# A gated dynamic convolution in fp32: output matmuls split around the value matmuls, softmax loads cut by lane, equal short end groups

## The chip, the cores and the metric

One core of a Trainium2 chip runs the program. Its time is the device time of one execution in microseconds (us), lower is better. Five engines run side by side, each in its own program order: PE (TensorE, matmuls; PEld is its weight load), DVE (VectorE), ACT (ScalarE), POOL (GpSimd) and SP (SyncE, which here only issues DMAs). Sixteen DMA engines carry all transfers.

## The reference

`x` is (8, 4224, 192) fp32, `weight_gen` is (8, 4224, 8 heads, 7 taps). The seven taps of each position and head go through a softmax and weight the last seven positions of that head's 24 channels. The result `a` then goes through a gate and two matrix products:

```python
w = softmax(weight_gen, axis=-1)                       # 7 taps
a[b, s, h, :] = sum_k w[b, s, h, k] * x[b, s - 6 + k, h, :]
gate_pre[s]   = sum_j conv_w[j] * a[s - 4 + j]          # 5 taps, per channel
out = (sigmoid(gate_pre) * (a @ w_val)) @ w_out         # 192 x 192 each
```

## The kernel before

The sequence is cut into 36 **groups** of positions, all eight batches ("lanes") of a group together. Before, group 0 has 24 positions and the other 35 have 120 (`N0`, `starts`, L52).

*Softmax.* `weight_gen` is loaded in seven **parts** of 16 x R positions (`Softmax`, L183; R is 10, 14, 30, 30, 60, 60, 60). A part lies on 128 partitions with R + 6 positions of each. `load` (L198) issues it as one DMA per 16 or 8 chunks, the lanes as the outermost dimension: on SP for the first three parts, on POOL for the last four (two DMAs each for the 60s). DVE does max, subtract, sum, reciprocal and normalise in cuts of about 22 positions (`jobs`), ACT the exponential. `spread` (ACT, L254) writes the weights with zeros between them into `zt`, and `store` (L271) writes `zt` to a DRAM block. A block written for the first time gets whole rows of 736 B, zeros and all; one written again gets only the 288 B of data in each row. Of the 60-position parts, part 4 writes fresh blocks and parts 5 and 6 write used ones.

*A group's front.* `load_x` brings positions of `x`, `load_t` the skewed rows of a block into `tb` as eight DMAs onto 16 partitions each; both are issued by SP. `tb` is then a banded matrix. `bank` (PE, L331) multiplies it with `x`, 128 short matmul records for the four banks; `evac` (ACT) takes a bank to the rings `ringA` (128 channels) and `ringB` (64), and `move` (POOL, 12 DMAs) brings the strips of heads 6 and 7 to their places.

*A group's back, one group later.* `tap0` (ACT) and four `tap`s (DVE) for each of the channel groups A and B make `gate_pre`; `sigm` (ACT) the gate; `val` (PE, L403) the product with `w_val`; `gv` (DVE) the product of the two. Then, another group later, `omm(0)` and `omm(1)` (PE, L429), the two **output parts**, four lanes each, multiply with `w_out` into `po`, of which there is one buffer; `oev` (ACT, L458) copies `po` to `ot`, and `store` (SP, L463) writes it out. So `omm(1)` can start only when `oev(0)` has emptied `po`.

*Order.* The program is written with an explicit plan: `at(t, f)` and `stage(m, offset, f)` give each call a time, and the calls are made in the order of those times. Only the order on each engine survives; an engine takes its next instruction when that one's inputs are there. Before, PE's order in a group is bank, val, omm(0), omm(1) (`stage` offsets 0 to 2.8, 3.7, 8.3, 10.7 in L622 to L642). SP's order at a stage is `load_x`, eight `load_t`, then the output stores, with the z stores between. SP issues a DMA only when an earlier one of the same semaphore has landed; eight semaphores go round.

*Weights.* `w_val`, `w_out` and `conv_w` come as 64-bit words and are converted in 8 steps each on DVE and POOL (`convert_weights`, L125).

Of the kernel before, what the change touches and what calls it, by code (L numbers as in the profile page):

```python
# [7 lines left out]
FP32 = mybir.dt.float32  # L8
# [9 lines left out]
def tile_dynconv_gated_moe(  # L18
# [21 lines left out]
    P = 128  # L40
# [11 lines left out]
    N0 = S % NB  # L52
    starts = [0] + [N0 + NB * i for i in range(S // NB)]
# [11 lines left out]
    ZR = 14  # L65
# [113 lines left out]
    blocks = [Block(16 * 10, "za"), Block(16 * 14, "zb")] + [Block(480, f"z{i}") for i in range(4)]  # L179
# [3 lines left out]
    class Softmax:  # L183
# [3 lines left out]
        def __init__(self, r0, R, into, step):  # L187
            self.r0, self.R, self.n = r0, R, R + PAD
            self.into = into
            h = -(-self.n // 22)  # L190
            self.cut = [(self.n * k // h, self.n * (k + 1) // h) for k in range(h)]
            self.zc = [(c, min(c + step, R)) for c in range(0, R, step)]
            self.q = 16 // len(into)
            for i, b in enumerate(into):
                assert b.n == self.q * R
                where.append((r0 + i * self.q * R, b))

        def load(self):  # L198
            R, n, q = self.R, self.n, self.q
            self.wt = wpool.tile([P, self.ROWS, H, K], FP32, name="wt")[:, 0:n]  # L200
            self.mx = wpool.tile([P, self.ROWS, H], FP32, name="mx")[:, 0:n]
            flat = self.wt.rearrange("p r h k -> p (r h k)")
            eng = nc.sync if self.r0 < 864 else nc.gpsimd
            ends = self.r0 + 16 * R == S
            for i in range(len(self.into)):
                off = wg.offset + (self.r0 + i * q * R) * ROW
                p0 = i * L * q

                def part(l0, dims, np, c0, c1):
                    src = bass.AP(tensor=wg.tensor, offset=off + l0 * S * ROW + c0 * ROW,  # L210
                                  ap=[*dims, [1, (c1 - c0) * ROW]])
                    p = p0 + l0 * q
                    eng.dma_start(out=flat[p:p + np, c0 * ROW:c1 * ROW], in_=src)

                every = [[S * ROW, L], [R * ROW, q]]
                if ends and i == len(self.into) - 1:
                    nc.vector.memset(self.wt[P - Q:P, R:], 0.0)
                    part(0, every, L * q, 0, R)
                    part(0, [[S * ROW, L - 1], [R * ROW, q]], (L - 1) * q, R, n)
                    part(L - 1, [[R * ROW, q - 1]], q - 1, R, n)  # L220
                else:
                    part(0, every, L * q, 0, n)
# [48 lines left out]
        def store(self, c):  # L271


            a, b = self.zc[c]
            for i, blk in enumerate(self.into):
                d0 = blk.t[0, a, :]
                p = slice(i * L * self.q, (i + 1) * L * self.q)
                np = L * self.q
                if self.old[i]:
                    dst = bass.AP(tensor=d0.tensor, offset=d0.offset, ap=[[self.R * PITCH, np], [PITCH, b - a], [1, DATA]])  # L280
                    nc.sync.dma_start(out=dst, in_=self.z[p, 0:b - a, 0:DATA])
                else:
                    dst = bass.AP(tensor=d0.tensor, offset=d0.offset, ap=[[self.R * PITCH, np], [1, (b - a) * PITCH]])
                    nc.sync.dma_start(out=dst, in_=self.z[p, 0:b - a].rearrange("p r c -> p (r c)"))

        def begin(self):
            self.old = [b.used for b in self.into]
            for b in self.into:
                b.used = True


    class Group:

        def __init__(self, m):
# [5 lines left out]
            self.p0 = HALO + NB * (m % 3) + NB - self.n  # L300
# [373 lines left out]
```

## Time and profile before

| what | before |
|---|---|
| time, median of 3 runs | 636.42 us (636.29 to 644.36) |
| profiled execution, time | 636.85 us |
| its span, first to last instruction | 634.9 us |
| PE busy | 507.0 us, 80% |
| DVE / ACT / POOL busy | 420.8 / 323.8 / 263.8 us |
| DMA bytes moved | 112.02 MB, 176 GB/s mean |

The span leaves out 1.95 us of the execution's time. A busy share is an average over a start-up, some thirty like groups and an end, so what sets the time has to be read stage by stage. "DMA share" is the mean busy share of the 16 DMA engines by the packets' own durations; packets overlap a little, so it can pass 1. "PEclk" is the granted TensorE clock as a share of full speed.

### The profile page before, as it was taken

What the parts mean: (1) busy time and instruction counts of PE and PEld (TensorE: products, weight loads), DVE (VectorE), ACT (ScalarE), POOL (GpSimd) and SP (SyncE); (2) the same over time, 40 slices, a digit from 0 to 9 for tenths busy, and PEclk for the clock granted to TensorE, in tenths of its full rate; (3) what the DMA queues carried; (4) which work ended last, traced back from release to release, by engine and by line L of the source; (5) the groups of instructions that cost most, each with busy time, mean ns of one, the idle gap of its engine ahead of it and who ended that gap; (6) DMA issues with size and microseconds to landing.
All of it is one profiled execution on the core that took longest, in us unless ns stands there. A gap on an engine that the chain in (4) does not pass through costs nothing. (4 is left out here: it accounts for less than half of the span.)

```text
span 634.9 us, 15917 instructions
## 1 busy us (share of the span) xinstructions
PE 507.0 (80%) x6324; PEld 334.1 (53%) x6324; DVE 420.8 (66%) x470; ACT 323.8 (51%) x521; POOL 263.8 (42%) x474
## 2 busy tenths in 40 slices
PE   7022799598986873999998569999998899999985
PEld 4022545465553553665565445655655566665553
DVE  7263386578886852788888375788885565566661
ACT  7031366455693632469566433694655444554431
POOL 7544244244444421445544252455444444445510
PEclk9556789899999876999999798999999999999998
DMA  6838479989869998687889894778897777777413
GB/s 161 184 113 181 89 250 179 203 219 246 188 127 202 256 242 242 139 178 162 192 196 214 182 229 112 165 166 192 194 207 179 165 166 165 182 167 164 111 53 93
DMA packets 128829, 112.02 MB, mean 176 GB/s; under 512 B 38742, under 2 KB 125922, under 8 KB 127604
## 3 DMA queue, kind: packets, MB, share of 16 engines
q1 hardware_dynamic: 112964, 96.33, 64.2%
q0 software_dynamic: 15792, 14.68, 11.4%
q8 instruction: 50, 0.82, 0.6%
q14 instruction: 23, 0.19, 0.1%
HBM read 60.46 MB, written 44.54 MB: 165 GB/s over the span
## 5 line engine op out<-in xcount | busy, mean ns | idle before, releaser
L369 POOL DMA_DIRECT2D ringA<-S x288 | 155.8, 548 | 265.5 <-ACT ringA L361 205.8
L396 DVE SCALAR_TENSOR_TENSOR aA<-ringA,wf,aA 128x960 f32<-128x960 f32 (+1 forms) x144 | 170.7, 1185 | 137.8 <-ACT aA L389 128.4
L342 PE MATMUL pa<-tb,xt 126*32 126x120 f32 (+1 forms) x4608 | 145.1, 286 | 71.6 <-DMA out_dram<-ot 34.4
L342 PEld LDWEIGHTS pa<-tb,xt 126*32 126x32 f32 (+1 forms) x4608 | 134.7, 118 | 81.2 <-issue 47.1
L461 ACT COPY ot<-po 120x768 f32<-120x768 f32 (+1 forms) x72 | 57.8, 802 | 186.0 <-PE po L440 141.2
L440 PE MATMUL po<-wf,aA 128*120 128x192 f32 (+1 forms) x576 | 114.0, 342 | 32.3 <-ACT ot L461 32.3
L440 PEld LDWEIGHTS po<-wf,aA 128*120 128x120 f32 (+1 forms) x576 | 91.6, 188 | 52.4 <-ACT ot L461 43.2
L371 POOL DMA_DIRECT2D ringB<-S x144 | 78.1, 547 | 61.6 <-DMA ringA<-S 34.5
L396 DVE SCALAR_TENSOR_TENSOR aB<-ringB,wf,aB 128x480 f32<-128x480 f32 (+1 forms) x144 | 101.3, 704 | 2.8 <-ACT aB L389 1.7
L411 PE MATMUL v<-ringA,wva 128*128 128x480 f32 (+1 forms) x144 | 68.9, 600 | 9.1 <-DMA ringA<-S 9.1
L447 PE MATMUL po<-wf,aB 64*120 64x192 f32 (+1 forms) x576 | 66.6, 349 | 2.1 <-DVE aB L427 2.1
L425 DVE TENSOR_TENSOR aA<-v,aA 128x960 f32<-128x960 f32 (+1 forms) x36 | 40.8, 1134 | 36.9 <-ACT aA L401 36.7
L447 PEld LDWEIGHTS po<-wf,aB 64*120 64x120 f32 (+1 forms) x576 | 44.6, 183 | 36.2 <-issue 33.6
L269 ACT COPY zt<-wt 128x192 f32<-128x192 f32 (+2 forms) x92 | 37.5, 487 | 35.0 <-DVE wt L252 35.0
L414 PE MATMUL v<-ringB,wvb 64*128 64x480 f32 (+1 forms) x144 | 43.2, 622 | 6.2 <-DMA ringB<-S 6.2
L389 ACT ACTIVATE aA<-ringA,wf 128x960 f32<-128x960 f32 (+1 forms) x36 | 39.2, 1089 | 17.0 <-DMA ringB<-S 16.6
L361 ACT COPY S<-pa 128x480 f32<-128x480 f32 (+1 forms) x36 | 19.9, 553 | 47.4 <-PE pa L342 47.4
L411 PEld LDWEIGHTS v<-ringA,wva 128*128 128x128 f32 x144 | 25.1, 196 | 32.5 <-issue 30.3
L419 PE MATMUL v<-ringB,wvd 128*128 128x480 f32 (+1 forms) x72 | 39.1, 626 | 0.0
L417 PE MATMUL v<-ringA,wvm 128*64 128x480 f32 (+1 forms) x144 | 37.3, 598 | 0.9 <-DVE aB L427 0.9
L361 ACT COPY ringA<-pa 128x480 f32<-128x480 f32 (+1 forms) x72 | 35.9, 546 | 1.2 <-PE pa L342 1.2
L401 ACT ACTIVATE aA<-aA 128x960 f32<-128x960 f32 (+1 forms) x36 | 35.6, 990 | 1.1 <-DVE aA L396 1.0
(60 smaller groups left out, 337.8 us busy)
## 6 DMA issues: line engine op xcount, KB each, us to landing
xt<-in_x_dram SPq DMA_DIRECT2D x35, 756.0 KB
out_dram<-ot SPq DMA_DIRECT2D x140, 180.0 KB
tb<-z SPq DMA_DIRECT2D x192, 88.0 KB
z<-zt SPq DMA_DIRECT2D x6, 920.0 KB
z<-zt SPq DMA_DIRECT2D x10, 552.0 KB
wt<-in_weight_gen_dram POOLq DMA_DIRECT2D x5, 924.0 KB, 15.3
ringA<-S POOLq DMA_DIRECT2D x280, 15.0 KB, 4.7
z<-zt SPq DMA_DIRECT2D x20, 216.0 KB
```

The lines of the kernel that those rows point to most:

```text
L342: nc.tensor.matmul(out=pa[Q * c:Q * c + Q, n * l:n * l + n], lhsT=self.xb[0:k, LH * u + l, C * h:C * h + Q], rhs=self.t[0:k, LH * u + l, P ...
L361: nc.scalar.copy(out=dst, in_=pa)
L369: nc.gpsimd.dma_start(out=ringA[q:q + h, LH * u:LH * u + LH, p0:p0 + n], in_=self.S[p:p + h])
L371: nc.gpsimd.dma_start(out=ringB[HD * u + q:HD * u + q + h, :, p0:p0 + n], in_=self.S[p:p + h])
L389: nc.scalar.activation(out=self.lanes(self.acc(g)), in_=self.src(g, 0), func=AF.Copy, scale=cw[:, g, 0:1])
L396: nc.vector.scalar_tensor_tensor(out=a, in0=self.src(g, j), scalar=cw[:, g, j:j + 1], in1=a, op0=ALU.mult, op1=ALU.add)
L411: nc.tensor.matmul(out=v01[:, u, 0:w], lhsT=wva, rhs=A[u], start=True, stop=False)
L414: nc.tensor.matmul(out=v01[:, u, 0:w], lhsT=wvb[hs], rhs=Bt[hs], start=False, stop=True, tile_position=(HD * u, 0))
L425: nc.vector.tensor_tensor(out=a, in0=self.v01[:, :, 0:w], in1=a, op=ALU.mult)
L440: nc.tensor.matmul(out=po[0:n, u, D * t:D * t + D], lhsT=gA[:, u, k, t], rhs=woa, start=first and t == 0, stop=not first, skip_group_check ...
L447: nc.tensor.matmul(out=po[0:n, u, D * t:D * t + D], lhsT=gB[hs, k, t], rhs=wob[hs], start=first and t == 0, stop=not first, skip_group_che ...
L461: nc.scalar.copy(out=self.ot[0:n], in_=self.po[0:n, :, 0:2 * D])
```

## The change

The short end groups become equal: `N0` is 72, so the groups have 72, 34 times 120, and 72 positions; there are still 36. The parts become R = 12, 16, 28, 28, 60, 60, 60, each with one block of its own, except that part 6 reuses part 4's block. So part 5 now writes whole rows. A fresh store is cut into runs of four rows (2,944 B) where it was one run of 10 or 12 rows (7,360 or 8,832 B).

A part is loaded lane by lane: eight DMAs of 16 partitions instead of one or two, all on SP (part 0 on SP and ACT in turn). The last three parts are also cut into three by position, so 24 DMAs, in three successive stages.

PE's order in a group becomes bank, omm(0), val, omm(1). `tap`s of B and A alternate; both `sigm` and both `gv` now fall into the group's own back stage, where B's came one later. Bank order is 3, 2, 0, 1 for 3, 0, 1, 2. The softmax jobs and the z stores get new places (three places for a store in a stage instead of two), and the start-up is written out by hand.

```diff
-    N0 = S % NB
+    N0 = (S % NB + NB) // 2
...
+    ZR = 12
+    ZQ = 4
...
+    blocks = [Block(16 * R, f"z{i}") for i, R in enumerate((12, 16, 28, 28, 60, 60))]
...
+        def load(self, l, c0, c1, eng):
...
+            src = wg.offset + (l * S + self.r0) * ROW
...
+                    s = bass.AP(tensor=wg.tensor, offset=src + c0 * ROW, ap=[[R * ROW, q], [1, (c1 - c0) * ROW]])
+                    eng.dma_start(out=flat[16 * l:16 * l + q, c0 * ROW:c1 * ROW], in_=s)
...
+            step, n = (PITCH, DATA) if self.old else (ZQ * PITCH, ZQ * PITCH)
...
+    for i, R in enumerate((12, 16, 28, 28, 60, 60, 60)):
+        parts.append(Softmax(r0, R, blocks[i if i < 6 else 4]))
...
+        if i > 3:
+            at(when(m - 2) + 4.0, s.tiles)
+            for c, (a, b) in enumerate(s.cut):
+                for l in range(L):
+                    at(when(m - 2 + c) + 4.1 + 0.5 * l, s.load, l, a, b, nc.sync)
+        else:
+            at(when(m - 1) + 6.0, load_all, s, (nc.sync,))
...
-        for i, kind in enumerate((3, 0, 1, 2)):
+        for i, kind in enumerate((3, 2, 0, 1)):
...
-        stage(m + 1, 3.7, g.val)
-        stage(m + 2, 2.7, g.sigm, 1)
-        stage(m + 2, 4.0, g.gv, 1)
-        stage(m + 2, 8.3, g.omm, 0)
-        stage(m + 2, 10.65, g.oev, 0)
+        stage(m + 1, 9.2, g.sigm, 1)
+        stage(m + 1, 10.4, g.sigm, 0)
+        stage(m + 1, 6.05, g.val)
+        stage(m + 1, 11.7, g.gv, 1)
+        stage(m + 1, 12.4, g.gv, 0)
+        stage(m + 2, 3.7, g.omm, 0)
+        stage(m + 2, 6.2, g.oev, 0)
...
         stage(m + 2, 10.7, g.omm, 1)
```

## Rows read from the trace of the kernel before

**Rows 1.** The page's head and its part 1: busy time and instructions of each engine

```profile
span 634.9 us, 15917 instructions
PE 507.0 (80%) x6324; PEld 334.1 (53%) x6324; DVE 420.8 (66%) x470; ACT 323.8 (51%) x521; POOL 263.8 (42%) x474
```

**Rows 2.** Windows by stage; columns: stretch, length, busy us (instructions) per engine, PEclk, DMA share, GB/s

```profile
0.00:89.30 89.30, 42.06 (x505) 26.30 (x505) 46.02 (x63) 33.01 (x60) 44.99 (x70) 0.68 0.64 154
89.30:266.80 177.50, 140.91 (x1742) 95.02 (x1740) 123.28 (x133) 95.33 (x152) 67.33 (x124) 0.91 0.88 207
266.80:495.80 229.00, 201.52 (x2616) 132.57 (x2615) 169.52 (x184) 135.04 (x215) 99.61 (x184) 0.98 0.82 184
495.80:595.20 99.40, 93.18 (x1222) 61.17 (x1223) 62.97 (x70) 46.37 (x75) 45.40 (x84) 1.00 0.73 166
595.20:634.90 39.70, 29.28 (x254) 19.00 (x252) 18.99 (x22) 14.03 (x20) 6.47 (x12) 0.94 0.25 73
```

**Rows 3.** Timeline of PE over one group: start, us, line, idle before and releaser

```profile
309.04 3.66 PE L342 MATMUL pa<-tb,xt 126*32 126x120 f32 x128
312.62 1.88 PE L411 MATMUL v<-ringA,wva 128*128 128x480 f32 x4
...
317.39 0.92 PE L447 MATMUL po<-wf,aB 64*120 64x192 f32 x8
...
320.70 1.57 PE L440 MATMUL po<-wf,aA 128*120 128x192 f32 x8 [0.89 <-ACT ot L461]
...
323.05 3.66 PE L342 MATMUL pa<-tb,xt 126*32 126x120 f32 x128
```

**Rows 4.** Waits of PE: waiter, releaser, us in total, times, longest us

```profile
PE pa L342 <- DMA out_dram<-ot: 34.4, 6, 8.9
PE po L440 <- ACT ot L461: 32.3, 36, 1.2
```

**Rows 5.** Timeline round one stall of PE: POOL, SP and PE

```profile
102.25 1.14 POOL L213 DMA_DIRECT2D wt<-in_weight_gen_dram  x2
102.54 19.12 SPq L325 DMA_DIRECT2D tb<-z  x8
...
124.28 5.45 PE L342 MATMUL pa<-tb,xt 126*32 126x120 f32 x128 [6.65 <-DMA out_dram<-ot]
...
308.72 7.66 SPq L325 DMA_DIRECT2D tb<-z  x8
```

**Rows 6.** Windows in which one kind of transfer runs nearly alone; columns as in Rows 2

```profile
14.00:16.00 2.00, 0.00 (x0) 0.00 (x0) 1.97 (x3) 1.47 (x4) 0.67 (x1) 0.90 0.48 151
18.00:20.00 2.00, 0.00 (x0) 0.00 (x0) 0.00 (x0) 0.25 (x1) 1.36 (x3) 0.50 1.04 335
24.00:26.00 2.00, 0.31 (x24) 0.34 (x27) 1.83 (x9) 0.00 (x0) 0.00 (x0) 0.50 1.19 136
30.00:34.00 4.00, 0.00 (x0) 0.00 (x0) 1.66 (x4) 0.00 (x0) 2.45 (x3) 0.50 0.54 123
```

**Rows 7.** DMA issues by line: count, KB each, us from issue to landing where known

```profile
z<-zt SPq DMA_DIRECT2D x6, 920.0 KB
z<-zt SPq DMA_DIRECT2D x10, 552.0 KB
wt<-in_weight_gen_dram POOLq DMA_DIRECT2D x5, 924.0 KB, 15.3
...
z<-zt SPq DMA_DIRECT2D x20, 216.0 KB
```

**Rows 8.** Timeline of the start-up: DVE, ACT and PE, with idle before and releaser

```profile
36.99 0.56 DVE L143 SCALAR_TENSOR_TENSOR wf<-raw,wf 128x384 uint32<-128x384 uint32 x1 [4.54 <-POOL wf L142]
...
41.69 1.86 ACT L269 COPY zt<-wt 128x224 f32<-128x224 f32 x4 [23.44 <-DVE wt L252]
...
43.88 0.64 PE L342 MATMUL pa<-tb,xt 30*32 30x24 f32 x32 [16.70 <-ACT S L361]
```

**Rows 9.** Windows over a group with two softmax jobs and one without; columns as in Rows 2

```profile
309.04:323.05 14.01, 13.12 (x176) 8.66 (x175) 11.25 (x14) 10.18 (x20) 6.48 (x12) 1.00 0.79 180
523.85:538.87 15.02, 14.13 (x176) 8.99 (x175) 9.11 (x11) 6.64 (x10) 6.48 (x12) 1.00 0.73 166
```

More of the change, by code (lines that the diff above doesn't have):

```diff
@@ L51, in tile_dynconv_gated_moe @@
     NB = 120
-    N0 = S % NB
-    starts = [0] + [N0 + NB * i for i in range(S // NB)]
+    N0 = (S % NB + NB) // 2
+    starts = [0] + [N0 + NB * i for i in range(-(-(S - N0) // NB))]
     NM = len(starts)
@@ L185, in tile_dynconv_gated_moe, with __init__ @@
         ROWS = 60 + PAD
-        def __init__(self, r0, R, into, step):
+        def __init__(self, r0, R, block):
             self.r0, self.R, self.n = r0, R, R + PAD
-            self.into = into
+            self.block, self.old = block, block.used
+            block.used = True
+            assert block.n == 16 * R
             h = -(-self.n // 22)
             self.cut = [(self.n * k // h, self.n * (k + 1) // h) for k in range(h)]
[L192 to L201, printed above, removed]
-            flat = self.wt.rearrange("p r h k -> p (r h k)")
[L203 to L222, printed above, removed]
@@ L274, in store @@
             a, b = self.zc[c]
[L275 to L289, printed above, removed]
+            d0 = self.block.t[0, a, :]
+            step, n = (PITCH, DATA) if self.old else (ZQ * PITCH, ZQ * PITCH)
+            dst = bass.AP(tensor=d0.tensor, offset=d0.offset,
+                          ap=[[self.R * PITCH, P], [step, (b - a) * PITCH // step], [1, n]])
+            if self.old:
+                src = self.z[:, 0:b - a, 0:DATA]
+            else:
+                src = self.z[:, 0:b - a].rearrange("p (r q) c -> p r (q c)", q=ZQ)
+            nc.sync.dma_start(out=dst, in_=src)
     class Group:
@@ L521, in tile_dynconv_gated_moe @@
+    at(10.5, lambda: clear(tb[0], cs, CELLS, 0, LH, nc.scalar))
     at(0.9, lambda: stir(60))
-    engs = {"DVE": nc.vector, "POOL": nc.gpsimd}
-    t = 14.5
-    for cs, w in ((slice(2 * D, NWT), "DVE"), (slice(0, D), "POOL"), (slice(D, 2 * D), "POOL")):
-        for eng, f in convert_weights(cs, "DVE", w):
+    s = parts[0]
+    at(6.5, s.max, 0)
+    at(7.8, s.sub, 0)
+    at(9.1, parts[1].max, 0)
+    at(9.2, s.exp, 0)
+    at(10.4, s.sum, 0)
+    at(11.7, s.recip, 0)
+    at(12.9, s.norm, 0)
@@ new lines, in tile_dynconv_gated_moe @@
+    at(14.2, parts[1].sub, 0)
+    at(15.6, parts[1].exp, 0)
+    at(19.6, parts[1].sum, 0)
+    at(20.9, parts[1].recip, 0)
+    at(22.2, parts[1].norm, 0)
+    engs = {"DVE": nc.vector, "POOL": nc.gpsimd}
+    for k, (c, w) in enumerate(((slice(2 * D, NWT), "DVE"), (slice(0, D), "POOL"), (slice(D, 2 * D), "POOL"))):
+        for i, (eng, f) in enumerate(convert_weights(c, "DVE", w)):
+            if k == 0:
+                t = 15.5 + 0.2 * i
+            elif eng == "POOL":
+                t = 16.0 + 5.0 * (k - 1) + i
+            else:
+                t = 17.0 + 1.3 * (k - 1) + 0.1 * i if i < 7 else (24.0, 29.4)[k - 1]
@@ L527, in tile_dynconv_gated_moe, with place_z @@
             at(t, lambda f=f, eng=eng: f(engs[eng]))
-            t += 0.01
-        t += 0.6
     for i, f in enumerate(place_weights()):
-        at(20.0 + 0.4 * i, f)
+        at(24.6 + 0.35 * i, f)
+    def place_z(s, c, t):
+        at(t, s.spread, c)
+        at(t + 0.1, s.store, c)
+        s.ready = t + 0.1
+    place_z(parts[0], 0, 14.1)
+    for c in range(2):
+        place_z(parts[1], c, 23.6 + c)
     def jobs(s):
@@ L619, in tile_dynconv_gated_moe @@
             stage(m - 1, 0.0, g.load_x)
-        need = [s.ready for s in parts if s.r0 < g.s + g.n]
-        at(max([when(m - 1) + 0.01 if m > 1 else 0.0, *(t + 0.01 + 0.01 * m for t in need)]), g.loads)
-        for i, kind in enumerate((3, 0, 1, 2)):
+        for i, j, lo, hi in g.segments():
+            t = max(when(m - 1) + 0.01 if m > 1 else 0.0, parts[i].ready + 0.01 * (m + 1))
+            assert t < when(m) - 5.0 or m < 2, (m, t, when(m))
+            at(t, g.load_t, i, j, lo, hi)
+        for i, kind in enumerate((3, 2, 0, 1)):
```

218 lines of the change are left out of this document (106 added, 112 removed).

## The prediction, made before the changed kernel was run

> **What bounds the kernel now.** I read the page's head first, for size alone. PE is busy 507.0 of 634.9 us and no other engine comes near it [rows 1], but such a share is an average, so the next view is the windows by stage, cut at bank starts of group 3, 13, 28 and 35 [rows 2]. Five stages appear: a start-up S of 89.3 us, then B, 177.5 us for 10 groups or 17.75 each, with DMA share 0.88; C, 229.0 us for 15 groups or 15.27 each, share 0.82; D, 99.4 us for 7 groups or 14.20 each, with no softmax left; and an end of 39.7 us.
>
> What does a group cost PE when nothing is late? The timeline of one says it: from bank start to bank start 323.05 - 309.04 = 14.01 us [rows 3]. The second output part lasts from 320.70 to 323.05, 2.35 us; the first, the same matmuls in another order, begins at 317.39 but the second begins 3.31 us later. So 3.31 - 2.35 = 0.96 us is a wait, and the row names it: `po` had to be emptied by ACT. The list of PE's waits gives it 36 times, with 32.3 us [rows 4]. Without it a group is 14.01 - 0.96 = 13.05 us of PE.
>
> The same list has a second wait: six stalls of a bank, 34.4 us [rows 4]. The releaser's name, an output store, is the last event on a queue and not the cause. Round one of them the timeline shows POOL issuing two loads of `weight_gen` at 102.25; the eight `tb` loads that SP starts right behind them take 19.12 us to issue, against 7.66 us in a quiet group, and the bank stands idle 6.65 us [rows 5]. The extra of B and C over 25 groups of 14.01 us (350.3) is 406.5 - 350.3 = 56 us, all of it of this kind or its aftermath: PE is off its full clock for 9% of B [rows 2].
>
> So: in D and quiet parts of C, PE with the `po` wait; in B, transfers; in S, a chain. In S ACT sits 23.44 us at the copy into `zt` for part 1, and behind it in ACT's order stands the evacuation of group 0, for which PE waits 16.70 us; DVE in turn was held by the weight conversion on POOL, 4.54 us here and as long once before [rows 8].
>
> **The change, part by part.**
>
> *Value between the output parts.* It removes nothing from PE's work. `oev(0)` now has the 4.77 us of `val` (312.62 to 317.39, [rows 3]) to empty `po`, and after `omm(1)` come 3.58 us of bank before the next `omm(0)`. ACT's copy would have to be over 4 us late to cost anything. Gain 0.96 us per group where PE is the bound: D becomes 7 x 13.05 = 91.4, say 92.
>
> *What is late next: DVE and ACT.* A group with two softmax jobs has 11.25 us on DVE and 10.18 on ACT; one without has 9.11 on DVE [rows 9]. Two jobs so cost some 2.1 to 2.9 us together, three up to 4.3, and DVE needs 9.1 + 4.3 = 13.4 in the three-job groups (B), 12.0 in the others. DVE thus holds 13.05 in C and D and is slightly over it in B, where the DMA takes longer anyway. The alternating taps and the earlier `sigm` and `gv` of B are the same instructions in another order: nothing, unless a chain of engines is late (rival 3).
>
> *DMA work per group.* D moves only x, `tb`, outputs and moves: 0.73 x 99.4 / 7 = 10.4 us of all sixteen engines [rows 2]. B has 0.88 x 177.5 = 156 us, 104 of it for its groups, so 52 for softmax traffic. C has 0.82 x 229.0 = 188, 156 for groups, 32 for softmax.
>
> *Loads by lane.* A 60-position part is 128 x 66 x 224 B = 1.89 MB. The window in which only such a load runs (part 2's) shows 123 GB/s at share 0.54: half the engines work [rows 6]. So a part costs 1.89/0.123 x 0.54 = 8.3 us of all engines, for 15.3 us [rows 7]. The new form is not in the trace. From below it runs like the widest transfer, a store from 128 partitions at 335 GB/s: 5.6 us. From above it runs like the only 16-partition transfer, the `tb` loads: 136 GB/s with every engine busy [rows 6]: 13.9 us. I take the middle, 9.8, for the rows are of 4,928 B, unlike either. What it does surely is end the starving: loads now stand in SP's own order behind x and `tb` of the next group, a third per stage, while before they pushed between them from POOL's queue. The eight more issues on SP in such a stage (0.5 us apart in the plan) stand in front of output stores, which have four buffers.
>
> [...]
>
> *Part 5 written fresh.* A fresh 60-position part is 128 x 60 x 736 B = 5.65 MB against 2.21 MB (10 x 216 KB). In B, 52 us less two loads of 8.3 leaves 35 for 8.5 MB (10 x 552 and 3 x 920 KB, [rows 7]), or 240 GB/s; in C, 32 - 8.3 = 24 us for two used parts, 12 each. So part 5 goes from 12 to 5.65/0.24 = 23.5 us, at best to 16.9 (335 GB/s).
>
> *B after*, 10 groups: 104 + two loads (11.3 to 27.8) + parts 3 and 4 fresh, 8.3 MB (24.7 to 34.5) = 140 to 166 us of DMA, middle 153, against 10 x 13.05 = 130.5 of PE. Transfers bound it still. At the share of before, 0.88, 153 becomes 174; I take 162, between that and no idleness, because x and `tb` are no longer starved.
>
> *C after*, 15 groups: PE 15 x 13.05 = 196. DMA 156 + one load (5.6 to 13.9) + part 5 (16.9 to 23.5) + part 6 (12) = 190 to 205. The two are level; at 0.88 the middle of 197 gives 224. I take 206, nearer the lower, since the need is spread evenly over the groups.
>
> *Start-up.* ACT's new order has the first evacuations ahead of part 1's spread, DVE does the reciprocal chain of part 1 ahead of the last conversion step, and part 0 covers groups 0 and 1. If the 23.44 us wait goes whole, group 3 begins at 89.3 - 23.4 = 66. Check by bytes: loads of parts 0 to 3 3.1 MB, x 2.8, `tb` 2.5, blocks of parts 0 and 1 2.6, weights 1.3, together 12.3 MB: 59 us at B's 207 GB/s, 80 us at the start-up's own 154 [rows 2]. I take 66, bounds 59 and 80.
>
> *End.* 39.7 us for two full groups; the last is now 0.6 of a full one, and B's gate no longer trails by a stage. I take 30, bounds 28 and 36.
>
> Sum: 66 + 162 + 206 + 92 + 30 = 556, and the 1.95 us outside the span: **558 us**. The base is the profiled execution, 636.85, which is 0.07% above the median 636.42.
>
> **Rivals.**
>
> 1. *Everything fits.* Lane loads and fresh stores at the wide rate: 62 + 141 + 197 + 91.5 + 29 + 2 = 523. For it: 335 GB/s exists [rows 6]. Against: nothing mixed reached it; B's mean is 207.
> 2. *The start-up does not shrink.* Another chain takes over (converted weights, moves that land late behind `tb` loads): 80 in place of 66, 572.
> 3. *A new chain replaces the `po` wait.* Gate and both `gv` must now end within one stage, so the period stays near 14: C 220, D 98, B 165, 581. Against: 12.0 of 13.05 on DVE leaves a little room.
> 4. *No change to measure.* DMA total before is 0.76 of the span, 484 us. With all lane loads at the `tb` rate (8.8 MB, 64.5 for 38.6 us) and part 5 at +11.5 it is 521. If share cannot pass 0.82, the time is 521/0.82 = 635.
> 5. *Slower.* The same work with share stuck at the present 0.76: 521/0.76 = 686; it decides from share 0.80 downward (651). Place: banks waiting for `tb` behind lane loads in SP's queue. For it: 24 to 26 us shows sixteen engines full at 136 GB/s [rows 6]. Against: B already runs at 0.88.
>
> [...]
>
> **From this to the numbers.** Chances: forecast 0.52, rival 1 0.15, rival 2 0.12, rival 3 0.12, rival 4 0.05, rival 5 0.04. Faster by over 2% (about what a measurement here can tell from no change; below 624) holds the first four, 0.91. All lower bounds add to 516, all upper ones (B 166/0.88, C 205/0.88) to 635; the range that leaves out 4 and 5 and the outer tails of the others is 522 to 605. The likeliest case alone spans 537 to 583.
>
> **What would show it.** The rows of the second output part without an idle before them, and D at 13.05 to 13.2 per group. No `tb` issue row of 19 us. Loads of `weight_gen` on SP's queue; a window with one alone, near 136 or near twice 123 GB/s, decides their price. Group 3's bank at 59 to 80 us. DMA share in B over 0.93. Wrong would be: stalls of banks in C longer than 15 us in sum (rivals 3 to 5), or D above 13.5.

## The result, and the profile of the changed kernel

The changed kernel takes 604.02 us (596.75 to 605.71), 0.942 of the kernel before (95% interval 0.932 to 0.952); measured again beside the last experiments it was 601.09 us, 0.944 (0.936 to 0.951). So it is faster by some 36 us. The forecast was 558, a gain of 78; the time lies inside the range of 522 to 605, only 1 us below its upper end, and less than half of the expected gain came. Its profiled execution is its fastest, 596.75 us, so the stages below add up to a gain of 40 us, a few more than the medians show.

The page's head and its part 1, kernel after (busy time, share and instructions of each engine); [rows 1] are those of before:

```profile
span 595.0 us, 15932 instructions
PE 489.3 (82%) x6324; PEld 337.2 (57%) x6324; DVE 422.0 (71%) x470; ACT 316.8 (53%) x517; POOL 257.8 (43%) x465
```

Windows of the kernel after, cut at the same bank starts as [rows 2]; columns as there:

```profile
0.00:72.20 72.20, 40.41 (x507) 26.51 (x508) 49.97 (x62) 33.55 (x60) 43.69 (x69) 0.74 0.86 188
72.20:239.00 166.80, 134.93 (x1742) 94.38 (x1740) 127.14 (x137) 93.23 (x153) 64.89 (x120) 0.92 0.90 231
239.00:468.10 229.10, 200.31 (x2616) 138.72 (x2617) 167.27 (x183) 130.48 (x210) 97.30 (x180) 0.95 0.84 199
468.10:562.70 94.60, 89.89 (x1224) 61.47 (x1222) 60.59 (x68) 46.46 (x75) 45.41 (x84) 1.00 0.74 163
562.70:595.00 32.30, 23.81 (x254) 16.09 (x252) 17.07 (x23) 13.08 (x20) 6.47 (x12) 1.00 0.26 76
```

Against [rows 2]: S 89.3 to 72.2, B 177.5 to 166.8, D 99.4 to 94.6, End 39.7 to 32.3. C, the longest stage, is 229.0 before and 229.1 after. Nothing came there, though 23 us were forecast; that is the question of this study.

PE over one quiet group of the kernel after, to be read against [rows 3]:

```profile
481.40 3.69 PE L335 MATMUL pa<-tb,xt 126*32 126x120 f32 x128
485.02 0.92 PE L440 MATMUL po<-wf,aB 64*120 64x192 f32 x8
...
487.28 1.77 PE L404 MATMUL v<-ringA,wva 128*128 128x480 f32 x4
...
491.85 1.46 PE L433 MATMUL po<-wf,aA 128*120 128x192 f32 x8
493.25 0.92 PE L440 MATMUL po<-wf,aB 64*120 64x192 f32 x8
494.10 0.32 PE L335 MATMUL pa<-tb,xt 126*32 126x120 f32 x4
```

No idle stands before either output part, and the group lasts 494.10 - 481.40 = 12.70 us, less than the 13.05 forecast. The 0.35 us below the forecast lie in the rows of `val` (4.57 us for 4.77) and of the output parts (2.26 and 2.25 for 2.35); they were not foreseen, and why these rows are shorter was not asked. So the main mechanism works: a group of PE's work with nothing late fell from 14.01 to 12.70. Fifteen of these are 190.5 us, and C takes 229.1.

Waits of PE in the kernel after (waiter, releaser, us in total, times, longest), against [rows 4]:

```profile
PE pa L335 <- DMA tb<-z: 36.7, 4, 19.1
PE pa L335 <- ACT S L354: 27.7, 15, 7.5
PE pa L335 <- DMA out_dram<-ot: 19.3, 7, 7.3
PE pa L335 <- DMA wt<-in_weight_gen_dram: 9.2, 3, 5.0
PE po L433 <- ACT ot L454: 2.3, 4, 0.9
```

The `po` wait of 32.3 us in 36 is 2.3 in 4. A new one stands in the list, a bank that waits for ACT's copy into `S`, which empties a bank's buffer, 27.7 us in 15. The three rows whose releaser is a DMA are banks that wait for `tb`; the 19.1 us is group 0 in the start-up, and 15.87 us of the same row is group 11, in B. In C alone, summed from PE's timeline: waits for `tb` went from 9.1 us in 3 to 18.4 in 6, for `S` from 0 to 9.0, for `po` from 13.6 to 0.4. PE's busy time in C is 200.3 us and not 190.5, because it works at a lower granted clock after each of the five waits of 2.48 us and more (PEclk is 0.95 in C and 1.00 in D; in the bank behind such a wait it is 0.50 to 0.69; the bank after the wait of 5.01 us takes 5.72 us at 0.60, against 3.69 above at 1.00). 190.5 + 9.8 of slower work + 28.8 of waits is the 229.1.

Timeline of the kernel after round its longest wait in C, at group 19, the first that reads part 5 (SP and PE):

```profile
327.86 0.34 SPq L281 DMA_DIRECT2D z<-zt  x1
...
328.74 3.23 SPq L322 DMA_DIRECT2D tb<-z  x4
...
335.96 4.96 PE L335 MATMUL pa<-tb,xt 126*32 126x120 f32 x128 [7.29 <-DMA out_dram<-ot]
```

The store at 327.86 is the last of part 5. The four `tb` loads that read it are issued behind it, with one group's time left. Groups 11 (15.87 us, in B) and 27 (3.64 us) look the same; they are the first readers of parts 4 and 6. Of the other four `tb` waits of C the longest, 5.01 us at group 18, has a z store and lane loads of the stage before in front of its loads.

Timeline of ACT and PE in the kernel after, round a wait for `S` in D:

```profile
506.76 2.84 PE L335 MATMUL pa<-tb,xt 126*32 126x120 f32 x96
507.13 0.62 ACT L394 ACTIVATE aB<-aB 128x480 f32<-128x480 f32 x1 [3.82 <-DVE aB L389]
508.26 1.02 ACT L394 ACTIVATE aA<-aA 128x960 f32<-128x960 f32 x1 [0.52 <-DVE aA L389]
...
510.10 0.69 ACT L382 ACTIVATE aB<-ringB,wf 128x480 f32<-128x480 f32 x1
510.70 0.54 ACT L354 COPY S<-pa 128x480 f32<-128x480 f32 x1
...
511.29 1.04 PE L335 MATMUL pa<-tb,xt 126*32 126x120 f32 x32 [1.69 <-ACT S L354]
```

`pa`, into which a bank is multiplied, has three buffers, so the fourth bank can start only when ACT has copied the first to `S`; here it waits 1.69 us for that. ACT is late with the copy: the gates wait for DVE (3.82 and 0.52 us), and the first tap of the group before (0.69 us at 510.10) stands in front of it too.

### The profile page after: what moved, and what is told of

It reads as the page before. It is cut to its first block, busy times and chain, and to the rows that moved or that the text cites. A ratio compares the mean times of both kernels' runs of the same rounds, so it can differ in the third digit from the quotient of the medians.

```text
span 595.0 us, 15932 instructions
## 1 busy us (share of the span) xinstructions
PE 489.3 (82%) x6324; PEld 337.2 (57%) x6324; DVE 422.0 (71%) x470; ACT 316.8 (53%) x517; POOL 257.8 (43%) x465
## 3 DMA queue, kind: packets, MB, share of 16 engines
q1 hardware_dynamic: 108637, 106.20, 72.8%
## 4 chain that ended last, share of the span: by engine, by line
DMA 39%; issue 16%; PE 15%; POOL 10%; DVE 9%; ACT 6%; SPq 4%; ACTq 0%; DVEq 0%; POOLq 0%
DMA ringA<-S 11%; DMA ringB<-S 11%; POOL ringA L362 8%; DMA tb<-z 6%; DMA xt<-in_x_dram 6%; PE pa L335 6%; DVE aA L389 5%; PE po L433 4%; SPq L322 2%; DMA wt<-in_weight_gen_dram 2%; PE po L440 2%; DVE aB L389 2%; DMA out_dram<-ot 2%; POOL ringB L364 2%; DMA z<-zt 1%
## 5 line engine op out<-in xcount | busy, mean ns | idle before, releaser
L389 DVE SCALAR_TENSOR_TENSOR aA<-ringA,wf,aA 128x960 f32<-128x960 f32 (+1 forms) x144 | 171.4, 1190 | 97.4 <-ACT aA L382 75.5
L335 PE MATMUL pa<-tb,xt 126*32 126x120 f32 (+1 forms) x4608 | 150.9, 291 | 93.2 <-DMA tb<-z 36.7
L335 PEld LDWEIGHTS pa<-tb,xt 126*32 126x32 f32 (+1 forms) x4608 | 137.4, 120 | 106.5 <-issue 57.1
L389 DVE SCALAR_TENSOR_TENSOR aB<-ringB,wf,aB 128x480 f32<-128x480 f32 (+1 forms) x144 | 100.6, 699 | 30.9 <-ACT aB L382 27.9
L433 PE MATMUL po<-wf,aA 128*120 128x192 f32 (+1 forms) x576 | 109.6, 333 | 2.9 <-ACT ot L454 2.3
L433 PEld LDWEIGHTS po<-wf,aA 128*120 128x120 f32 (+1 forms) x576 | 93.4, 186 | 28.0 <-issue 20.4
L404 PE MATMUL v<-ringA,wva 128*128 128x480 f32 (+1 forms) x144 | 64.5, 568 | 2.1 <-DMA ringA<-S 2.1
L382 ACT ACTIVATE aA<-ringA,wf 128x960 f32<-128x960 f32 (+1 forms) x36 | 38.9, 1081 | 46.4 <-DMA ringB<-S 35.2
L394 ACT ACTIVATE aB<-aB 128x480 f32<-128x480 f32 (+1 forms) x36 | 21.5, 598 | 74.4 <-DVE aB L389 74.3
L267 ACT COPY zt<-wt 128x192 f32<-128x192 f32 (+1 forms) x96 | 38.5, 480 | 18.0 <-DVE wt L250 9.9
L407 PE MATMUL v<-ringB,wvb 64*128 64x480 f32 (+1 forms) x144 | 38.7, 614 | 0.0
L404 PEld LDWEIGHTS v<-ringA,wva 128*128 128x128 f32 x144 | 26.5, 194 | 18.4 <-issue 17.6
```

What stands on the lines that cost most here:

```text
L335: nc.tensor.matmul(out=pa[Q * c:Q * c + Q, n * l:n * l + n], lhsT=self.xb[0:k, LH * u + l, C * h:C * h + Q], rhs=self.t[0:k, LH * u + l, P ...
L382: nc.scalar.activation(out=self.lanes(self.acc(g)), in_=self.src(g, 0), func=AF.Copy, scale=cw[:, g, 0:1])
L389: nc.vector.scalar_tensor_tensor(out=a, in0=self.src(g, j), scalar=cw[:, g, j:j + 1], in1=a, op0=ALU.mult, op1=ALU.add)
L394: nc.scalar.activation(out=a, in_=a, func=AF.Sigmoid)
L404: nc.tensor.matmul(out=v01[:, u, 0:w], lhsT=wva, rhs=A[u], start=True, stop=False)
L433: nc.tensor.matmul(out=po[0:n, u, D * t:D * t + D], lhsT=gA[:, u, k, t], rhs=woa, start=first and t == 0, stop=not first, skip_group_check ...
```

## The experiments

All are edits of the changed kernel unless said otherwise. "Ratio" is to the kernel before; stages are read from each profile at the bank starts of groups 3, 13, 28 and 35; the last two columns are PE's waits for `tb` and for `S` in C.

| kernel | us | ratio (95%) | S | B | C | D | End | tb | S wait |
|---|---|---|---|---|---|---|---|---|---|
| before | 636.42 | 1 | 89.3 | 177.5 | 229.0 | 99.4 | 39.7 | 9.1 | 0 |
| after | 604.02 | 0.942 (0.932-0.952) | 72.2 | 166.8 | 229.1 | 94.6 | 32.3 | 18.4 | 9.0 |
| after_again | 601.09 | 0.944 (0.936-0.951) | 74.1 | 167.8 | 229.0 | 97.3 | 32.0 | 21.2 | 7.4 |
| e1 | 637.08 | 0.999 (0.994-1.005) | 87.1 | 184.3 | 233.1 | 96.1 | 35.2 | 14.3 | 12.0 |
| e2 | 625.37 | 0.985 (0.978-0.992) | 77.8 | 167.0 | 238.2 | 105.8 | 35.0 | 8.3 | 0 |
| e3 | 621.18 | 0.975 (0.966-0.985) | 79.5 | 176.8 | 230.0 | 94.2 | 34.5 | 25.2 | 5.8 |
| e4 | 607.24 | 0.951 (0.942-0.959) | 72.8 | 165.3 | 234.4 | 93.9 | 34.6 | 25.1 | 6.3 |
| e5 | 590.00 | 0.930 (0.921-0.939) | 72.9 | 167.5 | 226.4 | 90.7 | 30.9 | 25.5 | 2.1 |
| e7 | 585.65 | 0.922 (0.912-0.931) | 74.1 | 172.8 | 216.7 | 89.2 | 31.9 | 14.8 | 3.9 |
| e8 | 589.82 | 0.929 (0.920-0.937) | 73.6 | 165.2 | 217.8 | 97.6 | 31.8 | 12.5 | 6.5 |
| e9 | 585.29 | 0.920 (0.913-0.927) | 72.0 | 168.8 | 219.6 | 91.4 | 30.9 | 19.2 | 1.7 |
| e11 | 607.85 | 0.954 (0.944-0.964) | 72.0 | 169.4 | 235.4 | 97.4 | 35.0 | 20.2 | 7.4 |
| e12 | 590.61 | 0.926 (0.917-0.935) | 73.3 | 171.9 | 219.2 | 89.9 | 31.1 | 15.4 | 5.4 |
| e13 | 584.76 | 0.914 (0.904-0.923) | 72.6 | 168.6 | 222.9 | 89.4 | 30.9 | 21.5 | 4.2 |
| e15 | 593.25 | 0.928 (0.920-0.937) | 73.1 | 169.7 | 222.3 | 95.8 | 33.8 | 16.6 | 4.1 |
| e17 | 580.48 | 0.913 (0.907-0.919) | 71.9 | 167.7 | 213.5 | 93.1 | 31.1 | 3.1 | 12.8 |
| e16 | 575.66 | 0.906 (0.899-0.912) | 71.8 | 167.3 | 212.3 | 94.2 | 30.9 | 0 | 4.5 |
| e19 | 572.50 | 0.897 (0.888-0.906) | 73.3 | 166.1 | 207.3 | 92.6 | 30.9 | 3.3 | 4.2 |

The two profiles of the changed kernel agree on C to 0.1 us but differ by 1.9 us in S and 2.7 in D, so differences of a stage below some 3 us are not read as effects here.

### What each part of the change is worth

**e1: the kernel before, with the group's new order alone.** The loop that plans a group's stage is that of the changed kernel; loads, blocks and parts are untouched.

```diff
-        for i, kind in enumerate((3, 0, 1, 2)):
+        for i, kind in enumerate((3, 2, 0, 1)):
...
-        stage(m + 2, 8.3, g.omm, 0)
+        stage(m + 2, 3.7, g.omm, 0)
```

> The kernel before with nothing of the change but the plan of a group's stage: bank order 3, 2, 0, 1 with its evacuations and moves, alternating taps, both gates in one stage, value between the output parts. If the PE order's gain needs nothing else: the po wait (32.3 us in 36) goes, D falls from 99.4 to 91 to 95, quiet groups from 14.0 to 12.7, and the whole is 606 to 614. If transfers hand it back in B and C as they did in the changed kernel's C: D still falls by 5 to 8, C by less than 8, the whole is 618 to 628. If softmax jobs, planned for the old order, now stand in front of the gates: 630 or more.

No gain at all. Waits of PE in e1:

```profile
PE pa L342 <- ACT S L361: 52.3, 14, 17.2
PE pa L342 <- DMA out_dram<-ot: 40.7, 10, 9.4
```

The `po` wait is gone here as well and D and End are shorter by 3.3 and 4.5 us, but the wait for `S` takes 52.3 us (32 of them in the start-up, 12.0 in C) and the waits for `tb` grew from 34.4 to 40.7 [rows 4]; B and C became longer by 6.8 and 4.1. The time falls where the third case of the expectation put it, and in part for its reason: ahead of the copies that end the two longest waits for `S` in C, at 290.52 and 418.98 us (3.43 and 3.09 us long), ACT has an exponential of the softmax in its order.

**e2: the changed kernel with value ahead of both output parts again.**

```diff
-        stage(m + 1, 6.05, g.val)
+        stage(m + 1, 3.7, g.val)
...
-        stage(m + 2, 3.7, g.omm, 0)
-        stage(m + 2, 6.2, g.oev, 0)
+        stage(m + 2, 8.3, g.omm, 0)
+        stage(m + 2, 10.65, g.oev, 0)
```

> The changed kernel with value back ahead of the first output part (plan times 3.7 for value, 8.3 for the first part, 10.65 and 10.66 for its copy and store). The po wait comes back with some 0.96 us a group where PE is the bound: D grows from 94.6 to 98 to 100, the whole by 5 (if B and C are bound elsewhere) to 25 us (if everywhere): 609 to 629.

Waits of PE in e2:

```profile
PE po L433 <- ACT ot L454: 54.9, 36, 3.9
PE pa L335 <- POOL wf L137: 18.1, 1, 18.1
```

The wait is back, 54.9 us in 36, and the time is 21 us longer: D by 11.2, C by 9.1, S by 5.6. D is beyond the 98 to 100 expected, since the wait is 1.5 us a group and not 0.96; in the new order ACT has gates ahead of the copy. So value's place between the output parts is worth 21 us here, where the whole new order of the group gave nothing in the kernel before; the two edits are not the same, e1 moves banks, taps and gates as well.

**e3: each set of eight lane loads as one load again**, lanes outermost, on SP at the same places.

```diff
-                    s = bass.AP(... ap=[[R * ROW, q], [1, (c1 - c0) * ROW]])
+                    s = bass.AP(... ap=[[S * ROW, L], [R * ROW, 16], [1, (c1 - c0) * ROW]])
```

> The changed kernel with each set of eight lane loads made one load again, lanes outermost as in the kernel before, but on SP and in thirds: 3 issues for a part where there were 24. If the lane form brings engines (the sixteen that work on a lane load against half before), the single load at 123 GB/s takes longer to land (a third of 0.63 MB some 5 us) and C and B grow: 608 to 620. Theory A (eight open transfers): 21 places fewer per part, C falls by 8 to 15 us, 588 to 598, in spite of the slower loads. Theory B (bytes): no difference, 600 to 608; start-up longer by some us, since parts 0 to 3 are loaded this way too.

The lane form is worth some 17 us, nearly all of it in S (7.3) and B (10.0); C is the same to 1 us. The packet records of the two traces show how much of a load is in flight: in the kernel before, part 2's load in [rows 6] has 8 packets of 8,064 B at a time, at moments 9; in the kernel after, the lane load issued at 188.56 us has 16 packets of 4,928 B, 10 of them at once at 192.77 us.

**e11: the lane loads of parts 4 to 6 on POOL's queue**, behind the stage's moves.

```diff
-                    at(when(m - 2 + c) + 4.1 + 0.5 * l, s.load, l, a, b, nc.sync)
+                    at(when(m - 2 + c) + 4.8 + 0.01 * l, s.load, l, a, b, nc.gpsimd)
```

> The changed kernel with the lane loads of parts 4 to 6 issued by POOL right behind its moves of the same stage, not by SP; same pieces, same stages, same bytes. Looked at closer, each issue of SP in the trace of the changed kernel begins when the eighth transfer before it has landed: SP waits 100.4 us in 30 waits on an x load at a tb issue, and 9.2 us on x at a weight_gen issue. Theory A (eight open transfers on SP are the limit in C; 24 lane loads of a part take places that tb, outputs and z need): C falls from 229 to 205 to 218, B by some us too, the whole is 575 to 594. Theory B (the bytes of fresh stores and loads that fall together are the limit, whoever issues them): C stays at 222 to 232, the whole is 598 to 606. Theory C (as in the kernel before, packets from POOL's queue starve tb): tb issue rows over 12 us beside the loads, 610 or more.

Theory A is not borne out: SP is rid of 72 issues, and C is not shorter (235.4). e3 says the same, with 21 issues fewer for a part and C at 230. Neither run is clean, for the loads themselves changed queue or form with it; e19 below is the better witness, see the last section. Theory C shows only weakly: the longest `tb` issue in C takes 13.32 us (10.09 in the changed kernel).

**e4: part 6 written fresh too.**

```diff
-    blocks = [Block(16 * R, f"z{i}") for i, R in enumerate((12, 16, 28, 28, 60, 60))]
+    blocks = [Block(16 * R, f"z{i}") for i, R in enumerate((12, 16, 28, 28, 60, 60, 60))]
```

> The changed kernel with a block of its own for part 6 too, so that its five stores write whole rows (1104 KB each) in place of the 432 KB of a used block, in stages 22 to 26. The prediction priced one part written fresh at 23.5 us of all engines against 12 used, 11.5 more. If C is bound by its bytes: C grows by 8 to 12 us, 612 to 616. If a store costs C only when it stands in front of a tb load (theory D): the fresh store, 5 to 6 us from issue to landing against 4 to 6 for the used one, costs hardly more, C grows by 0 to 4, 604 to 608.

Window of stage C in e4:

```profile
238.10:472.50 234.40, 201.59 (x2615) 140.75 (x2613) 166.82 (x182) 130.76 (x210) 97.31 (x180) 0.93 0.85 210
```

C is 5.3 us longer, by its profile, while the two times cannot be told apart (the intervals overlap). The DMA work is 0.85 x 234.4 = 199.2 against 0.84 x 229.1 = 192.4 us: a part written fresh costs some 6.8 us more of all engines (the shares are rounded, so 5 to 9).

### What holds C

**e5: on ACT, the first taps behind the evacuations.**

```diff
-        stage(m + 1, 0.85, g.tap0, 1)
-        stage(m + 1, 2.65, g.tap0, 0)
+        stage(m + 1, 2.2, g.tap0, 1)
+        stage(m + 1, 4.4, g.tap0, 0)
```

> The changed kernel with one move in ACT's order: the first tap of group B of channels comes behind the evacuation of S and of ringB (2.2 instead of 0.85 in the plan), the first tap of group A behind both evacuations of ringA (4.4 instead of 2.65); the second taps on DVE follow (2.95 and 5.2). The changed kernel has 604.0 us, stages S 72.2, B 166.8, C 229.1, D 94.6, End 32.3. Theory 1 (a chain over ACT makes the groups long: a bank waits for ACT to empty S, 27.7 us in 15 waits, and ACT stands in front of a tap that waits for moves to land): this wait goes, D falls from 94.6 to 90 or less, C by some 15 us, the whole by 15 to 25 us to 580 to 590. Theory 2 (bursts of transfers make C long, and ACT only waits along): C stays within 5 us of 229, D gains at most 3, the whole is 596 to 604.

Each theory is half right. The wait for `S` goes (9.0 to 2.1 in C) and D falls to 90.7, 12.96 a group. But C stays at 226.4: what PE no longer waits for `S` it waits for `tb` (18.4 to 25.5).

**e8: the loads of parts 5 and 6 two and five stages earlier.**

```diff
-                    at(when(m - 2 + c) + 4.1 + 0.5 * l, ...
+            d = (0, 0, 0, 0, 2, 4, 7)[i]
+                    at(when(m - d + c) + 4.1 + 0.5 * l, ...
```

> The changed kernel with the weight_gen loads of part 5 in stages 6 to 8 instead of 8 to 10, and those of part 6 in stages 11 to 13 instead of 16 to 18, so that they no longer stand in the stages in which the previous part's fresh 12-row chunks are written. The number of bytes is the same. Theory 2 (bursts): the stall ahead of group 11 (PE 2.4 us busy of 18.3 between 193 and 212 us) and those between 283 and 336 us (periods of 17.8 and 22.1 us) shrink; C falls from 229.1 by 12 to 20 us, B may pay 3 us for the loads in stages 6 to 8, the whole is 587 to 596. Theory 1 (the ACT chain): C falls by less than 5 us, the whole is 600 to 606. Theory 3 (C is bound by the sum of its transfers, whatever their order): the bytes of part 6's load stay inside C, so C stays at 224 to 229.

C falls by 11 us, and the whole by 14 with the same bytes. Not all of the 11 is order: stages 11 and 12 lie in B, so 16 issues of part 6's lane loads left C, and its DMA work fell from 192.4 to 0.86 x 217.8 = 187.3 us. B took them up without growing (165.2 for 166.8). So where the transfers stand matters; that their sum is not the limit (theory 3) is shown more cleanly by e12.

**e9: e5 and e8 together.**

> Both moves together: first taps on ACT behind the evacuations, and loads of parts 5 and 6 in the earlier stages. If chain and bursts are two separate costs, the gains add: 604 - 20 - 14 = 570 us, with C near 196 to 202 and D near 89. If one hides the other (groups that no longer wait for ACT then wait for transfers), the sum is less than the larger of the two plus 5 us: 585 to 595.

The gains do not add: C 219.6, with 19.2 us of waits for `tb`.

**e7: no output stores of groups 13 to 27.**

```diff
+            if 13 <= self.m < 28:
+                return
             h = self.n // 2
```

> The changed kernel without the output stores of groups 13 to 27 (30 stores a kind left out, so that part of the output isn't written); all else is unchanged. Theory 2 and 3 (transfers bind C): with some 11 MB, about 33 us of sixteen engines at 335 GB/s, taken out, C falls from 229.1 to 195 to 205 us. Theory 1 (ACT chain): C falls by 10 us at most, to 219 or more, since nothing on ACT waits for an output store that has four buffers.

Window of stage C in e7:

```profile
246.90:463.60 216.70, 198.03 (x2612) 137.69 (x2610) 167.39 (x184) 130.44 (x210) 96.97 (x180) 0.96 0.79 173
```

Of the 11 MB left out some 8 fall into C. The DMA share there is 0.79, and C is still 216.7 with 14.8 us of waits for `tb`, 5.88 of it at group 19; that is neither the 195 to 205 of theories 2 and 3 nor the 219 of theory 1. Fewer bytes help, by 12 us, but a stage whose DMA engines are idle a fifth of the time still waits for transfers: that is lateness, and not volume alone.

**e12: x and `tb` loads planned 8.15 us earlier**, right after the bank that frees the buffer.

```diff
-            stage(m - 1, 0.0, g.load_x)
+            stage(m - 2, 4.9, g.load_x)
...
-            t = max(when(m - 1) + 0.01 if m > 1 else 0.0, parts[i].ready + 0.01 * (m + 1))
+            t = max(when(m - 2) + 4.91 if m >= 4 else ..., parts[i].ready + 0.01 * (m + 1))
```

> The changed kernel with the x and tb loads of groups 4 and up planned 8.15 us earlier: at 4.9 us into the stage two before their bank (right after the bank that frees the tb buffer) and so ahead of that stage's softmax stores, instead of at the start of the stage just before. Bytes, pieces and order on PE, DVE and ACT are unchanged. Theory D (C's stalls come from tb loads that have one group's time to be issued and to land, so that a z store of 5 us or some lane loads ahead of them make their bank late although the average over C has room): the waits of a bank for tb (18 us of C by their rows, and some 8 us of lower clock after them) mostly go, C falls from 229 to 205 to 214, B by 5 to 10, the whole is 575 to 590. Theory B (bytes in total are the limit while they last): C 224 to 230, the whole is 600 to 606. Theory E (SP now waits longer for PE to free tb, and outputs and stores wait behind it): 606 or more.

Timeline of e12, SP and PE, round group 19:

```profile
323.91 0.41 SPq L299 DMA_DIRECT2D xt<-in_x_dram  x1
324.41 0.81 SPq L281 DMA_DIRECT2D z<-zt  x1
...
335.21 2.18 PE L335 MATMUL pa<-tb,xt 126*32 126x120 f32 x37 [11.53 <-DMA tb<-z]
```

Window of stage C in e12:

```profile
245.20:464.40 219.20, 196.40 (x2612) 135.01 (x2610) 167.09 (x184) 129.72 (x210) 97.59 (x181) 0.96 0.88 206
```

C is 219.2, and its DMA work, 0.88 x 219.2 = 192.9 us, is that of the changed kernel (192.4): the same work in 10 us less. B did not fall by the 5 to 10 us expected (171.9 for 166.8). Of six waits for `tb` in C two are left, 11.53 us at group 19 and 3.83 at group 27. Both are first readers of a part: their loads cannot move ahead of the part's last store, at 324.41 here.

**e13: e12, e5 and e8 together.**

> The three moves together: x and tb loads 8.15 us earlier, the first taps on ACT behind the evacuations, and the loads of parts 5 and 6 in stages 6 to 8 and 11 to 13. Theory D: the late tb loads that the first two left in place (19 us of waits in C when both were made) go too; C 195 to 205, D 89 to 91, the whole is 555 to 570. Theory B: as with the two moves, 582 to 588.

The same two waits, now 14.42 and 7.04 us; C is 222.9 and the time 584.76, far from the 555 to 570 of theory D. PE only comes earlier to the same store: part 5's last store is issued at 324.80 us (324.41 in e12), and PE stands idle from 321.3 us instead of 323.7.

**e15: part 5 finished three stages earlier**, by three softmax jobs a group up to group 15.

```diff
-    per = {m: 3 if m < 11 else 2 for m in range(2, NM + 2)}
+    per = {m: 3 if m < 16 else 2 for m in range(2, NM + 2)}
```

> The changed kernel with three softmax jobs in a group up to group 15 instead of up to group 10, so that part 5's five fresh stores stand in stages 13 to 15 and not in 14 to 18, the last of them three stages ahead of its first use instead of one. Theory F (the part's late end is what hurts: its last store and the pieces of tb at its border stand in front of group 19's bank): the stall of 7.3 us there and the lower clock after it go, C falls by 8 to 12 us, 592 to 597. Theory B or D (the stores stand in front of some group's tb wherever they are): the stall moves to groups 14 to 16, C within 5 us of 229, 600 to 606; DVE with three jobs (13.4 us by the prediction's sum) is a little over the period there, 2 us more.

By itself it mostly moves the waits: the period that ends with group 19's bank falls from 22.1 to 14.7 us, the one before group 17's rises from 12.7 to 18.6, and 16.6 us of waits for `tb` stay in C (222.3).

**e17: the lead (from group 13) and early parts 5 and 6 together.**

```diff
-    begins = {3: 2, 4: 5, 5: 10, 6: 18}
+    begins = {3: 2, 4: 5, 5: 10, 6: 16}
```

> The changed kernel with x and tb loads 8.15 us earlier from group 13 on, and with three softmax jobs a group up to group 15 and part 6 begun in group 16 instead of 18, so that the last stores of parts 5 and 6 stand in stages 15 and 24 and not in 18 and 26. ACT's order and the stages of part 5's loads are those of the changed kernel. Theory G (the last store of a part comes too late for its first reader, groups 19 and 27): with the lead in place nothing else is late, both long waits (11.5 and about 5 us and the lower clock after them) go, C falls from 229 to 198 to 206, the whole is 570 to 580. Theory B (bytes): C 215 to 222, the whole is 586 to 593.

The waits for `tb` in C go from 18.4 us to 3.1, where lead alone left 15.4 and an early part 5 alone 16.6. That settles what made banks late: both were needed. (Part 6's lane loads, begun with the part, also stand two stages earlier here; what they alone give at group 27 is not separated.)

Window of stage C in e17:

```profile
239.60:453.10 213.50, 197.63 (x2616) 136.44 (x2614) 164.33 (x181) 123.71 (x207) 97.07 (x180) 0.97 0.90 208
```

The DMA work is 0.90 x 213.5 = 192.2 us, again that of the changed kernel. C itself falls only to 213.5, not to 198 to 206: the waits for `S` grow to 12.8, and PE's work takes 7.1 us more than 190.5 at the lower clock.

**e16 and e19: with e5's and e8's moves as well**, e19 with three jobs only up to group 13 and part 6 begun in 17.

> As the run with lead and early parts, and besides the first taps on ACT behind the evacuations and the loads of part 5 in stages 6 to 8, of part 6 in 11 to 13. Theory G: C 193 to 200, D 89 to 91, the whole is 557 to 567. Theory B: C 215 to 222, the whole is 580 to 588.

> As the run with everything, but three softmax jobs a group only up to group 13 and part 6 begun in group 17, so that the last stores of parts 5 and 6 stand in stages 16 and 25. Theory G: still a full stage ahead of the first reader's loads, C within 3 us of the run with everything, with some 2 us less on DVE in groups 14 and 15: the whole is 556 to 567. If lateness is a matter of degree, the two long waits come back in part: C 205 to 212.

Windows of B, C and D in e19, the fastest kernel of the study, 0.897 of the kernel before (0.888 to 0.906):

```profile
73.30:239.40 166.10, 137.85 (x1740) 96.98 (x1740) 131.43 (x139) 97.97 (x156) 64.73 (x120) 0.92 0.92 234
239.40:446.70 207.30, 196.69 (x2616) 135.68 (x2614) 167.55 (x181) 126.28 (x208) 96.96 (x180) 0.98 0.90 213
446.70:539.30 92.60, 89.25 (x1221) 61.72 (x1219) 64.07 (x71) 49.88 (x77) 45.26 (x84) 1.00 0.78 173
```

C is 207.3 at a DMA share of 0.90, and 0.90 x 207.3 = 186.6 us of DMA work is about that of the changed kernel (192.4). The difference is in part lane loads of part 6, of which 10 fewer stand in C. Nearly the same work went into 22 us less. Theory G's 193 to 200 for C and its 556 to 567 for the whole were not reached in either; e19's C is in the 205 to 212 named for lateness as a matter of degree, but the waits for `tb` that came back are only 3.3 us. In e16 no bank waits for `tb` in C, but another chain shows (timeline, ACT and PE):

```profile
280.94 1.64 ACT L267 COPY zt<-wt 128x192 f32<-128x192 f32 x4 [9.80 <-DMA z<-zt]
283.32 1.96 PE L433 MATMUL po<-wf,aA 128*120 128x192 f32 x5 [7.12 <-ACT ot L454]
```

Two stores of 1104 KB close together keep both `zt` buffers; ACT waits 9.80 us to spread the next, and the copy that empties `po` stands behind it in ACT's order. In e19 the 16.8 us above 190.5 are 10.6 us of waits and 6.2 of work at a lower clock; they were not followed further.

**after_again: the changed kernel, on the chip of the last three.**

> The changed kernel itself, unchanged, on the chip of these runs: 597 to 606 us, with C at 229 to 235 and the same two or three long waits for tb at groups 11, 17 and 19.

C 229.0, with its long waits for `tb` at the same groups as in the first profile of the changed kernel (10.31 us at group 19); both have group 18, not the 17 of the expectation.

## Why the prediction was wrong

**Where the miss lies.** The profiled execution is 39 us above the forecast: C has 23 of them, S 6, B 5, D 3 and the end 2. Of the signs of being wrong both came: banks wait 27.4 us in C (18.4 for `tb`, 9.0 for `S`, where 15 was the limit), and D is 13.51 us a group, just over the limit of 13.5.

**Value between the output parts: right, and a little better than said.** 12.70 for 13.05. e2 prices it at 21 us in the changed kernel.

**C, 206: wrong, and the step that failed is one clause:** "nearer the lower, since the need is spread evenly over the groups". The volume was right: 197 us of DMA work in the middle, 192.4 measured (0.84 x 229.1). The share was not: 206 needs 0.96 of 197, and the stage went on at 0.84, as before at 0.82. The sentence before it has nearly the number that came, 224 at a share of 0.88.

The need is even over fifteen groups but not over one: the ten z stores of C stand in groups 15 to 18 and 23 to 26, one or two in each, and the `tb` of a group has one group's time to be issued and to land behind them. The sum over a stage asked whether the transfers fit; it did not ask when each is due. A shorter PE period makes that due time earlier, so that the 13.2 us won at `po` came back as 9.3 us more waiting for `tb` and 9.0 for `S`. e1 agrees: the new order in the kernel before raises the waits for `tb` in C from 9.1 to 14.3 us. e12, e15 and e17 show it: with loads issued earlier and parts finished earlier the waits for `tb` go to 3.1 us, and C with the same DMA work to 213.5; with part of the work moved to B as well it is 207.3 in e19. Part 5 written fresh is a rival that no run undid in the changed kernel; but e1, where that part is not fresh, has C at 233.1, and e12 and e17 shorten C with the fresh writes in place, so they alone are not what kept C at 229.

**The rivals.** Rival 3 (a new chain takes the `po` wait's place) was half right, with another place: not gates that end late for the output, but ACT's copy into `S` behind gates and a first tap. It explains D, 94.6 against 92 (e5 brings 90.7), and 9.0 us of C. Rivals 4 and 5 put a stuck share as a property of the transfers; the share did stick in C, but 0.90 in e17, at the same DMA work, shows that the order set it.

**S, 66: off by 6, inside its bounds of 59 and 80.** The ACT wait of 23.44 [rows 8] has become 7.66; group 1's fourth bank still waits 7.52 us for ACT. By bytes 188 GB/s x 72.2 us is 13.6 MB where the sum had 12.3.

**B, 162: 166.8.** Its DMA work is 0.90 x 166.8 = 150 us for a forecast of 153, so the work was right and the share again too high: 162 needs 0.94. The sign named for it, a share over 0.93, did not come. The prediction also read PEclk 0.91 in B before as 9% of the time off the full clock; windows of B before show full clock and half (PEclk 1.00 in 130 to 200 us, 0.50 in 203.5 to 210), so a mean of 0.91 is half clock for about 18% of B. No term of the sum rests on it. Here the longest `tb` issue of B is 9.69 us where it was 19.12 [rows 5]. Group 11, the first reader of part 4, alone waits 15.87.

**Lane loads, 9.8 us of all engines a part: right size.** Windows of the kernel after in which the lane loads of part 1 make most of the traffic:

```profile
9.00:11.00 2.00, 2.00 (x14) 1.26 (x13) 1.97 (x2) 2.00 (x1) 0.00 (x0) 1.00 0.95 164
11.00:13.00 2.00, 1.26 (x9) 0.59 (x6) 0.01 (x1) 1.96 (x2) 0.00 (x0) 1.00 0.57 127
```

1.89/0.127 x 0.57 = 8.5 and 1.89/0.164 x 0.95 = 10.9. Part of it is weights on POOL's queue: SP's queue, which carries the lane loads, moved 0.23 MB in the first window at a share of 0.66 and 0.22 MB in the second at 0.50, some 115 and 110 GB/s. So they go no faster than the 123 GB/s at 0.54 of [rows 6], and these two windows do not show the near twice 123 GB/s that the prediction named as one of two prices; no run has one lane load alone. Where the 17 us of e3 come from in detail stays open.

**Part 5 fresh, 11.5 us more than used: 6.8 by e4**, near the lower bound of 16.9 - 12 = 4.9. e4 measured it on part 6.

**End, 30: 32.3,** inside its bounds of 28 and 36. PE waits there 1.17 us for `S` and twice 0.9 us for `po`.

## What to carry to other kernels

A wait taken off the engine that bounds a stage shortens the period (14.01 to 12.70 us here), and with it the time that every transfer has between its issue and its use: ask of each load how many periods ahead it is issued, and what stands in front of it, before adding up whether the bytes fit. Look for the first reader of each batch of produced data; its due time is set by the producer's last store, and no earlier issue helps there (e12 left 11.53 and 3.83 us). A new order can be worth nothing alone (e1) while a part of it is worth 21 us beside the rest of the change (e2), so undo a part in the finished kernel as well as doing it alone.

## What the runs showed that was not expected

SP waits longest for landings: 100.4 us for those of `x`, at `tb` issues alone. Waits of SP's queue in the kernel after:

```profile
SPq L322 <- DMA xt<-in_x_dram: 100.4, 30, 5.2
...
SPq L281 <- DMA xt<-in_x_dram: 3.4, 1, 3.4
```

The last `tb` issue of a group waits for the landing of the group's own `x`, eight issues before it, 3.3 us on average. In C it is 42.6 us in 13 waits. e3 and e11 gave SP fewer issues, but left this wait as it was (43.3 and 47.7 us in C; 103.0 and 111.8 in the whole run); in e19's C it is 53.1 us while C is 22 us shorter. So it is not what held C at 229. A z store was held in the same way once, 3.4 us; what that costs was not tried by itself.
